# The last 64 rows of three weight matrices: sixteen long reads in place of 128 short ones

## The chip, the cores and the metric

The kernel runs on one core of a Trainium2 chip. The core has a matmul engine (PE, with PEld for its weight loads), a vector engine (DVE), an activation engine (ACT), a general engine (POOL) and a sequencer for transfers (SP), and sixteen DMA engines that move data between the chip's memory (HBM) and the on-chip memory (SBUF, 128 rows called partitions). The metric is the time of one launch in device microseconds, here as the median of three runs: lower is better.

## The reference

One decoding step for a batch of four: layer norm, attention of 32 query heads over a window of the last 4096 cached positions of 16 key/value heads, an output projection, a second norm and a gated feed-forward with ReLU as the gate. Cut to what is computed:

```python
B, Sq, D = 4, 1, 576;  Hq, Hkv, Sk, Dh = 32, 16, 16384, 128;  F = 4608;  W = 4096
xn = layernorm(x)
q = (xn @ wq)                                    # wq: 576 x 4096
k, v = k_cache[:, :, Sk - W:], v_cache[:, :, Sk - W:]    # each kv head serves two q heads
o = softmax(q k^T * Dh ** -0.5) v
h = x + o @ wo                                   # wo: 4096 x 576
hn = layernorm(h)
gate = hn @ W_gate;  gate = gate * (gate > 0)    # W_gate, W_up: 576 x 4608
h2 = h + (gate * (hn @ W_up)) @ W_down           # W_down: 4608 x 576
```

All tensors are bf16. Nearly all of the work is reading: the windows of K and V are 2 x 67 MB, the weights together some 25 MB. Every byte is read once.

## The kernel before

**Order by hand.** A small scheduler (class `Prog`) keeps one list of instructions for each engine and puts in semaphore waits from named dependencies. Nothing reorders the lists. All loads but that of x stand in SP's list; x's load and one of the two stores of the output are on ACT's.

**Memory.** One SBUF tensor `arena` (128 x 81,920 bf16) holds everything large. Its first 16,384 columns take q in a spread-out form, the rest are four slots of 16,384 columns (4 MB each). A load into a slot is issued by SP as soon as the last reader of what was there is done (`place`, L242, keeps an owner for every 64 columns). The loads in SP's order are: the last 64 rows of wq into `pp` (L251), its first 512 rows into a slot (L255), then K and V blocks of four heads each: K0 to K3, then K4, V0, K5, V1 and so on to K15, V11, then V12 to V15. After these come wo (L266), W_gate and W_up (L276), and W_down in five pieces (L282), laid over the arena as it falls free.

**Rows of the weights.** A weight of 576 rows is contracted in five chunks of 128 partitions. `main_rows` gives the first 512 rows to 128 partitions, four consecutive rows each, so a partition reads one contiguous run. `last_rows` gives the remaining 64 rows to 128 partitions by cutting each row in halves: partition 2r + a holds half a of row 512 + r. For wq that is a run of 2048 values (4,096 B) for each partition, for W_gate and W_up 2304 values (4,608 B). The matmuls use this layout through `xnT[:, 4:6]` and `hnT[:, 4:6]`, chunk 4 of the contraction, whose two columns are masked by `par` for even and odd partitions.

**Work.** PE projects q (L379 and L34, the helper `mm_same`). For each K block DVE transposes it in place (L422, 32 x 32 blocks), PE multiplies it with q (L446, L34); four blocks make a batch element, followed by a softmax (ACT and DVE). For each V block PE multiplies the weights with it (L507, L34) and DVE and ACT pick and add the heads' parts (L517 to L524). At the end come the output projection (L615), the second norm, the gate and up projections (L664, in the order W_gate, then W_up, chunk 4 first), the ReLU product and the down projection (L685), and two stores.

**What waits for the three loads.** wq's last rows (`("L", "wq", 1)`) are awaited by chunk 4 of the q projection, after the four main chunks. Those of W_gate (`("gu", 0, 4)`) and of W_up (`("gu", 1, 4)`) are issued ahead of the main part of the same matrix and are awaited by the first matmul of chunk 4 of that matrix.

Of the kernel before, what the change touches and what calls it, by code (L numbers as in the profile page):

```python
# [18 lines left out]
F = 4608  # L19
# [13 lines left out]
def mm_same(e, out, lhsT, rhs, start, stop, tile, pos):  # L33
    return e.add_instruction(mybir.InstMatmult(  # L34
        name=e.bass.get_next_instruction_name(), engine=mybir.EngineType.PE, ins=[e.lower_ap(rhs), e.lower_ap(lhsT)],
        outs=[e.lower_ap(out)], start_tensor_calc=start, stop_tensor_calc=stop, tile_size=tile, tile_position=pos,
        ldweights=False, bass_skip_group_check=True))


class Op:  # L40
# [80 lines left out]
def bass_sequential_preLN__sliding_block_cached__glu_gated_reglu__decode_kernel(  # L121
# [12 lines left out]
    with ExitStack() as es:  # L134
        cnt = [0]

        def sb(name, shape, dt):
            return es.enter_context(nc.sbuf_tensor("sb_" + name, shape, dt))

        P = Prog()  # L140
# [8 lines left out]
        arena = sb("arena", [128, AW], BF16)  # L149
# [44 lines left out]
        pT = pp[:, 0:4096]  # L194
# [21 lines left out]
        def place(name, off, size, reader, make, key=None):  # L216
            deps = []
            for blk in range(off // 64, (off + size) // 64):
                r = owner.get(blk)
                if r is not None and r not in deps:  # L220
                    deps.append(r)
                owner[blk] = reader
            semk = key or "d_" + "_".join(str(v) for v in name)
            P.dma("sync", ("L",) + name, make, semk, deps)
            land[name] = off
# [3 lines left out]
        def ring_slot():  # L229
            s = ring[0] % NSLOT  # L230
            ring[0] += 1
            return s
# [12 lines left out]
        def main_rows(W):  # L245
            return W[0:512, :].rearrange("(p r) n -> p (r n)", r=4)

        def last_rows(W):
            return W[512:576, :].rearrange("r (a n) -> (r a) n", a=2)

        P.dma("sync", ("L", "wq", 1), lambda e: e.dma_start(out=pT[:, 0:2048], in_=last_rows(A_wq)), "d_wq1")  # L251
        s = ring_slot()
        wq_off = slot0 + s * TILE
        place(("wq", 0), wq_off, TILE, "QMM",
# [12 lines left out]
        gu_off = {}  # L267
        off = WO_OFF + H * D
        for g, W in ((0, B_W_gate), (1, B_W_up)):
            for m, n, src in ((4, F // 2, last_rows(W)), (0, 3 * F, main_rows(W)[:, 0:3 * F]), (3, F, main_rows(W)[:, 3 * F:4 * F])):  # L270
                if g == 0 and m == 0:
                    n, src = 4 * F, main_rows(W)
                elif g == 0 and m == 3:
                    continue
                gu_off[(g, m)] = off
                place(("gu", g, m), off, n, ("GU", g, m), lambda e, off=off, n=n, src=src: e.dma_start(out=arena[:, off:off + n], in_=src))  # L276
                off += n
        WD_ROWS = (0, 15, 25, 32, 35, 36)
        wd_off = off
        for r0, r1 in zip(WD_ROWS, WD_ROWS[1:]):  # L280
            place(("wd", r0), wd_off + r0 * D, (r1 - r0) * D, ("DOWN", 1),
                  lambda e, r0=r0, r1=r1: e.dma_start(  # L282
                      out=arena[:, wd_off + r0 * D:wd_off + r1 * D],
                      in_=B_W_down.rearrange("(p r) n -> p (r n)", p=128)[:, r0 * D:r1 * D]))
# [18 lines left out]
                                                in_=c_qm[:, :, :].rearrange("p q (h j) -> p q h j", j=4),  # L303
# [4 lines left out]
                                                in_=to_v[:, :, :].rearrange("p n (k a) -> p n k a", a=4),  # L308
# [14 lines left out]
        for sg in range(2):  # L323
            pool(f"c_toq{sg + 1}", lambda e, sg=sg: e.affine_select(
                out=toq[:, :, :, :], in_=toq[:, :, :, :],
# [40 lines left out]
        def pe_q():  # L366
            for c in range(DC):
                for bk in range(2):
                    for g in range(4):
                        n = 4 * bk + g  # L370
                        w = arena[:, wq_off + c * H * DH + n * 512:][:, 0:512] if c < 4 else pT[:, g * 512:g * 512 + 512]
                        deps = []
                        if bk == g == 0:
                            deps = {0: [("L", "wq", 0), "xnT", "c_xnT"], 4: [("L", "wq", 1)]}.get(c, [])
                        if c < 4 and bk:
                            fn = lambda e, c=c, w=w, g=g, bk=bk: mm_same(e, bank[4 + bk][32 * g:32 * g + 32, :], xnT[:, c, :], w,
                                                                         c == 0, False, (128, 32), (0, 32 * g))
                        else:
                            fn = lambda e, c=c, w=w, g=g, bk=bk: e.matmul(  # L379
                                bank[4 + bk][32 * g:32 * g + 32, :], lhsT=xnT[:, c + bk if c == 4 else c, :], rhs=w,  # L380
                                start=(c == 0), stop=(c == 4), skip_group_check=True)
                        pe("QMM" if bk else "QMM0", fn, deps)
            for blk in range(8):
                pe("QT", lambda e, blk=blk: e.matmul(
                    bass.AP(tensor=psb, offset=7 * 512 + blk // 4 * 16 + blk % 4, ap=[[4096, 128], [4, 4], [32, 4]]),
                    lhsT=bass.AP(tensor=pp, offset=4096 + blk * 128, ap=[[PPW, 128], [1, 128]]),
                    rhs=bass.AP(tensor=ident_b, offset=0, ap=[[128, 128], [32, 4], [1, 4]]),
                    start=True, stop=True, skip_group_check=True), [f"qev{blk // 4}"] if blk % 4 == 0 else [])
# [36 lines left out]
        def pe_qk(g):  # L425
            b, qd = divmod(g, 4)
            for cb in range(4):
                for w in range(2):
                    for a in range(4):
                        deps = []  # L430
                        if cb == w == a == 0:
                            deps = [("TRA", g)]
                            if g == 0:
                                deps.append("QW")
                            if qd == 0 and b:
                                deps += [("EXP", b - 1), ("MAX", b - 1), ("EV", b - 1, 1)]
                        off = land[("K", g)] + w * QWW + cb // 2 * 64 + cb % 2 + a // 2 * 8 + a % 2 * 2
                        lhsT = arena[:, b * 2048 + cb * 512 + g % 4 * 128 + a * 32:][:, 0:32]
                        rhs = bass.AP(tensor=arena, offset=off, ap=[[AW, 128], [128, 64], [16, 4], [4, 2]])
                        out_ = bank[w][32 * a:32 * a + 32, :]  # L440
                        start, stop = g % 4 == cb == 0, g % 4 == cb == 3
                        if w:
                            fn = lambda e, a=a, out_=out_, lhsT=lhsT, rhs=rhs, start=start, stop=stop: mm_same(
                                e, out_, lhsT, rhs, start, stop, (128, 32), (0, 32 * a))
                        else:
                            fn = lambda e, out_=out_, lhsT=lhsT, rhs=rhs, start=start, stop=stop: e.matmul(  # L446
                                out_, lhsT=lhsT, rhs=rhs, start=start, stop=stop, skip_group_check=True)
                        pe(("QK", g), fn, deps)
# [90 lines left out]
        def finish_o():  # L539
            for q in range(4):  # L540
                for qd in range(4):
# [17 lines left out]
                                              in_=bass.AP(tensor=e8, offset=0, ap=[[8, 128], [0, 4], [1, 8]])), ["c_e8", "c_selc0"])  # L559
# [47 lines left out]
        for a in range(8):  # L607
            for n in range(2):
                for j in range(4):
# [4 lines left out]
                    else:  # L614
# [6 lines left out]
                                             in_=bass.AP(tensor=psb, offset=512 + 224, ap=[[4096, 128], [1, 64], [0, 2]])), ["part1"])  # L621
# [54 lines left out]
        for i in range(2):  # L676
            dve(("HHT", i), lambda e, i=i: e.transpose(
                out=hhT[:, 576 * i:576 * i + 576].rearrange("p (r q) -> p r q", q=32),
                in_=bass.AP(tensor=pp, offset=3712 + 18 * i, ap=[[PPW, 128], [1, 18], [36, 32]])), [("HH", m) for m in range(3)])
# [24 lines left out]
        for n in range(2):  # L704
            lo, hi = ncol[n]
            P.dma(("sync", "scalar")[n], ("O", n), lambda e, n=n, lo=lo, hi=hi: e.dma_start(
                out=orow[:, lo:hi], in_=out_sb[32 * n:32 * n + 4, 0:hi - lo]),
# [31 lines left out]
```

## Time and profile before

| what | value |
|---|---|
| median of 3 runs | 378.25 us (377.94 to 378.27) |
| span of the profiled execution | 376.5 us |
| DVE busy | 227.6 us (60%) |
| PE busy | 209.2 us (56%) |
| ACT busy | 53.8 us (14%) |
| mean DMA rate over the span | 424 GB/s |
| K loads, 16 of 4096 KB, issue to landing | 26.2 us (median) |
| V loads, 16 of 4096 KB, issue to landing | 28.5 us (median) |
| wq, first 512 rows, issued at 1.3 us | lands 12.9 us later |
| W_gate, first 512 rows, issued at 320.1 us | lands 29.3 us later |
| x, 4.5 KB, on ACT's queue, issued at 0.93 us | lands at 3.66 us |
| first matmul of the q projection (L379) | 14.21 us |
| first matmul of the gate projection (L664) | 353.56 us |

How to read the profile: one execution is recorded, and times are microseconds from the start of its span. The runs' times are taken without the profiler and by another clock, which takes in what lies around the span; they are close to it but not the same. "Landing" is the time when the last of the sixteen DMA engines has marked its share of a load as done. A DMA engine takes the shares of one queue in the order of their issue, each as a number of packets; the trace has start and duration of every packet, without the engine's number. "Busy" of an engine says nothing by itself: what counts is which wait ends last.

### The profile page before, as it was taken

The page shows a single profiled execution, that of the slowest core. Times are in us where ns is not written, and L with a number is a line of the kernel's source. Part 1 is how long each engine was busy: PE and PEld are TensorE (multiplying, and loading weights), DVE is VectorE, ACT ScalarE, POOL GpSimd, SP SyncE. Part 2 cuts the span into 40 slices and gives each one's busy share as a digit, 9 for nine tenths or more (in the row PEclk, how much of TensorE's full clock was granted, in tenths as well). Part 3 has the DMA queues.
Part 4 walks back from the last instruction along what each step waited for, and adds up shares of the span by engine and source line. Part 5 has one row for each costly group of instructions (what it writes and reads, how often), then busy time and mean ns, then how long its engine had stood idle before and what let it go on. Part 6 is the DMA issues. An engine that isn't in the chain of part 4 may idle for free.

```text
span 376.5 us, 2541 instructions
## 1 busy us (share of the span) xinstructions
PE 209.2 (56%) x1447; PEld 39.2 (10%) x694; DVE 227.6 (60%) x164; ACT 53.8 (14%) x84; POOL 10.7 (3%) x29
## 2 busy tenths in 40 slices
PE   0404443249919091749282844664555687776748
PEld 0000000001101010101010100110000101003305
DVE  3088878779292959584847778665659423342140
ACT  3093000211000114010101140101010401121010
POOL 8300000000000000000000000000000000000000
PEclk9975666659979687788778885968596989996688
DMA  8999999999999999999999999999999999999996
GB/s 335 446 435 432 413 446 446 425 411 446 444 421 414 443 444 421 414 446 446 421 413 446 446 418 421 438 446 418 425 439 446 413 432 435 430 423 426 437 414 263
DMA packets 6514, 159.74 MB, mean 424 GB/s; under 512 B 736, under 2 KB 872, under 8 KB 1512
## 3 DMA queue, kind: packets, MB, share of 16 engines
q1 hardware_dynamic: 6488, 159.58, 98.8%
q8 instruction: 8, 0.13, 0.1%
q10 hardware_dynamic: 16, 0.01, 0.0%
q14 instruction: 2, 0.02, 0.0%
HBM read 159.58 MB, written 0.00 MB: 424 GB/s over the span
## 4 chain that ended last, share of the span: by engine, by line
DMA 62%; DVE 18%; PE 18%; SPq 1%; issue 1%; ACT 0%
DMA sb_arena<-in_A_k_cache_dram 53%; DVE sb_arena L422 16%; PE psb L34 11%; DMA sb_arena<-in_B_W_down_dram 9%; PE psb L446 4%; PE psb L507 2%; DVE sb_o_tmp L520 1%; DVE sb_pp L485 1%; PE psb L685 0%; SPq L242 0%; PE psb L473 0%; SPq L282 0%; ACT sb_out_sb L702 0%; SPq L255 0%; SPq L251 0%
## 5 line engine op out<-in xcount | busy, mean ns | idle before, releaser
L422 DVE STREAM_TRANSPOSE sb_arena<-sb_arena 128x8192 f32<-128x8192 f32 (+1 forms) x19 | 139.9, 7365 | 66.5 <-DMA sb_arena<-in_A_k_cache_dram 66.5
L446 PE MATMUL psb<-sb_arena 128*32 128x512 bf16 x256 | 42.5, 629 | 119.1 <-DVE sb_arena L422 119.0
L34 PE MATMUL psb<-sb_arena,sb_pp 128*128 128x512 bf16 x382 | 105.2, 383 | 2.7 <-issue 2.6
L507 PE MATMUL psb<-sb_arena,sb_pp 128*128 128x512 bf16 x115 | 44.1, 383 | 8.9 <-DVE sb_o_tmp L520 8.9
L34 PE MATMUL psb<-sb_arena 128*32 128x512 bf16 x256 | 44.2, 649 | 0.0
L517 ACT COPY sb_o_tmp<-psb 32x512 f32<-32x512 f32 x32 | 18.5, 577 | 179.3 <-PE psb L34 179.1
L520 DVE TENSOR_TENSOR sb_o_tmp<-psb,sb_fm 32x512 f32<-32x512 f32 x32 | 21.7, 678 | 16.9 <-PE psb L34 16.4
L446 PEld LDWEIGHTS psb<-sb_arena 128*32 128x32 bf16 x256 | 9.6, 119 | 161.4 <-DVE sb_arena L422 132.2
L507 PEld LDWEIGHTS psb<-sb_arena,sb_pp 128*128 128x128 bf16 x128 | 12.6, 99 | 113.4 <-issue 113.4
L524 DVE TENSOR_REDUCE sb_o_sel<-sb_o_tmp 128x128 f32<-128x512 f32 x16 | 17.7, 1106 | 0.5
L465 ACT ACTIVATE sb_pp<-psb,sb_hx 128x1024 bf16<-128x1024 f32 x4 | 4.5, 1113 | 78.4 <-DVE sb_hx L462 78.4
L485 DVE TENSOR_TENSOR sb_pp<-psb,sb_m 128x1024 bf16<-128x1024 f32 x8 | 9.4, 1209 | 4.5 <-PE psb L473 4.5
L480 ACT ACTIVATE sb_pp<-psb,sb_m 128x512 bf16<-128x512 f32 x16 | 9.7, 692 | 14.8 <-PE psb L473 14.8
L523 DVE TENSOR_TENSOR sb_o_tmp<-sb_o_tmp,sb_fm 64x512 f32<-64x512 f32 x16 | 11.0, 690 | 0.5
L413 ACT COPY sb_arena<-sb_q_keep 32x256 bf16<-32x256 bf16 x8 | 9.7, 1452 | 0.1
L685 PE MATMUL psb<-sb_arena,sb_pp 128*32 128x352 bf16 (+1 forms) x72 | 7.6, 349 | 3.7 <-DMA sb_arena<-in_B_W_down_dram 3.6
L399 DVE CAST sb_pp<-psb 128x512 bf16<-128x512 f32 x1 | 2.4, 2426 | 11.3 <-PE psb L379 11.3
L468 DVE STREAM_TRANSPOSE sb_pp<-sb_pp 128x1024 bf16<-128x1024 bf16 x4 | 5.0, 1246 | 5.1 <-ACT sb_pp L465 5.1
L473 PE MATMUL psb<-sb_pp,sb_to_v 128*32 128x256 bf16 x64 | 4.3, 401 | 6.2 <-DVE sb_pp L468 6.2
L673 DVE TENSOR_TENSOR sb_pp<-psb,sb_pp 128x384 bf16<-128x384 f32 x3 | 1.5, 551 | 9.0 <-PE psb L664 9.0
L379 PE MATMUL psb<-sb_arena,sb_xnT 128*32 128x512 bf16 x16 | 2.6, 628 | 7.2 <-DMA sb_arena<-in_A_wq_dram 7.2
L664 PE MATMUL psb<-sb_arena,sb_hnT 128*32 128x384 bf16 x40 | 4.2, 405 | 3.9 <-DVE sb_hnT L645 2.0
(119 smaller groups left out, 88.1 us busy)
## 6 DMA issues: line engine op xcount, KB each, us to landing
sb_arena<-in_A_k_cache_dram SPq DMA_DIRECT2D x16, 4096.0 KB, 26.2
sb_arena<-in_A_v_cache_dram SPq DMA_DIRECT2D x16, 4096.0 KB, 28.5
sb_arena<-in_A_wo_dram SPq DMA_DIRECT2D x1, 4608.0 KB, 26.2
sb_arena<-in_B_W_gate_dram SPq DMA_DIRECT2D x1, 4608.0 KB, 29.3
sb_arena<-in_A_wq_dram SPq DMA_DIRECT2D x1, 4096.0 KB, 12.9
sb_arena<-in_B_W_up_dram SPq DMA_DIRECT2D x1, 3456.0 KB, 30.3
sb_arena<-in_B_W_down_dram SPq DMA_DIRECT2D x1, 2160.0 KB, 29.6
sb_arena<-in_B_W_down_dram SPq DMA_DIRECT2D x1, 1440.0 KB, 32.6
```

Source lines behind the costliest of these rows:

```text
L34: return e.add_instruction(mybir.InstMatmult(name=e.bass.get_next_instruction_name(), engine=mybir.EngineType.PE, ins=[e.lower_ap(rhs), e. ...
L413: act("QW", lambda e, i=i, q=q: e.copy(out=bass.AP(tensor=arena, offset=32 * i * AW + 2 * i + q, ap=[[AW, 32], [512, 16], [136, 4], [32, 4]]),
L422: dve(("TRA", g), lambda e: e.transpose(out=dst, in_=src), [("L", "K", g)] if lo == 0 else [])
L446: fn = lambda e, out_=out_, lhsT=lhsT, rhs=rhs, start=start, stop=stop: e.matmul(out_, lhsT=lhsT, rhs=rhs, start=start, stop=stop, skip_gr ...
L480: act(("EV", b, 0), lambda e, a=a: e.activation(out=bass.AP(tensor=pp, offset=2 * a, ap=[[PPW, 128], [8, 2], [32, 128], [1, 2]]), in_=bank ...
L485: dve(("EV", b, 1), lambda e, n=n: e.tensor_tensor(out=bass.AP(tensor=pp, offset=16 + 8 * n, ap=[[PPW, 128], [32, 128], [2, 4], [1, 2]]), ...
L507: fn = lambda e, lhsT=lhsT, rhs=rhs, k=k, j=j: e.matmul(bank[2 + j], lhsT=lhsT, rhs=rhs, start=(k == 0), stop=(k == 7), skip_group_check=True)
L517: act(("OSC", g), lambda e, j=j: e.copy(out=o_tmp[32 * j:32 * j + 32, 0:512], in_=bank[2 + j][32 * j:32 * j + 32, :]), [("PV", g), ("OSEL" ...
L520: dve(("OSD", g), lambda e, j=j: e.tensor_tensor(out=ot(32 * j, 32), in0=bank[2 + j][32 * j:32 * j + 32, :].rearrange("p (t d) -> p t d", ...
L523: dve(("OS", g), lambda e: e.tensor_tensor(out=ot(64, 64), in0=ot(64, 64), in1=fmb(64, 64), op=ALU.mult), [("OSC", g)])
L524: dve(("OSEL", g), lambda e: e.tensor_reduce(out=o_sel[:, qd, b, :], in_=o_tmp[:, 0:512].rearrange("p (t d) -> p d t", d=DH), axis=AX.X, o ...
L685: return lambda e: e.matmul(bank[n][32 * n:32 * n + 32, 0:hi - lo], lhsT=lhsT, rhs=w[:, lo:hi], start=start, stop=stop, skip_group_check=True)
```

## The change

Three loads are written differently: the last 64 rows of wq (L251), of W_gate and of W_up (L276, those with m = 4). The 64 rows lie in HBM as one contiguous stretch. Before, both sides of the transfer are 128 runs of half a row. After, the source is sixteen runs of four whole rows (32,768 B for wq, 36,864 B for W_gate and W_up), while the destination is still 128 partitions of a half row each, so one source run fills eight neighbouring partitions. Since partition 2r + a holds half a of row r, the bytes lie in SBUF exactly where they lay. The two sides now differ in shape, and a new helper `load_wide` adds the copy instruction directly, on SP's queue. Semaphores, waits, the order of issue and all other loads are as they were.

```diff
+def load_wide(e, out, in_):
+    return e.add_instruction(mybir.InstDMACopy(
+        name=e.bass.get_next_instruction_name(), engine=mybir.EngineType.SP, mode="Copy", queue="qSPDynamicHW",
+        ins=e.lower_ap_dma(in_), outs=e.lower_ap_dma(out)))
...
-        def last_rows(W):
-            return W[512:576, :].rearrange("r (a n) -> (r a) n", a=2)
-
-        P.dma("sync", ("L", "wq", 1), lambda e: e.dma_start(out=pT[:, 0:2048], in_=last_rows(A_wq)), "d_wq1")
+        def last_wide(W):
+            n = W.shape[1]
+            return bass.AP(tensor=W.tensor, offset=512 * n, ap=[[4 * n, 16], [1, 4 * n]])
+
+        P.dma("sync", ("L", "wq", 1), lambda e: load_wide(e, pT[:, 0:2048], last_wide(A_wq)), "d_wq1")
...
-            for m, n, src in ((4, F // 2, last_rows(W)), (0, 3 * F, main_rows(W)[:, 0:3 * F]), (3, F, main_rows(W)[:, 3 * F:4 * F])):
+            for m, n, src in ((4, F // 2, last_wide(W)), (0, 3 * F, main_rows(W)[:, 0:3 * F]), (3, F, main_rows(W)[:, 3 * F:4 * F])):
...
-                place(("gu", g, m), off, n, ("GU", g, m), lambda e, off=off, n=n, src=src: e.dma_start(out=arena[:, off:off + n], in_=src))
+                place(("gu", g, m), off, n, ("GU", g, m), lambda e, off=off, n=n, src=src, m=m: (
+                    load_wide(e, arena[:, off:off + n], src) if m == 4 else e.dma_start(out=arena[:, off:off + n], in_=src)))
```

## The prediction

> **What bounds the kernel now.** I read the page first: its slices, its DMA queues and its chain of waits.
>
> ```profile
> span 376.5 us, 2541 instructions
> ...
> DMA  8999999999999999999999999999999999999996
> GB/s 335 446 435 432 413 446 446 425 411 446 444 421 414 443 444 421 414 446 446 421 413 446 446 418 421 438 446 418 425 439 446 413 432 435 430 423 426 437 414 263
> ...
> q1 hardware_dynamic: 6488, 159.58, 98.8%
> q8 instruction: 8, 0.13, 0.1%
> ...
> DMA 62%; DVE 18%; PE 18%; SPq 1%; issue 1%; ACT 0%
> ```
>
> The reader should see that the 16 DMA engines are busy at 90% or more in 38 of 40 slices, and that the one queue SP fills (q1) accounts for 98.8% of their time. 159.58 MB at the rate of the long middle stage (below: 431 GB/s) is 370 us of 376.5. The chain names DVE and PE too, but they stand there because a slot is refilled only when its reader is done; loads wait about 26 us in the queue after issue (next views), so the DMA engines never run dry over it. A microsecond lost in the DMA stream anywhere is a microsecond at the end.
>
> Second, the stretch from the last weights to the end, in the chain in order of time, and what PE waited for there:
>
> ```profile
> 338.23 34.60 DMA sb_arena<-in_B_W_down_dram
> 372.83 0.04 issue
> 372.88 1.86 PE psb L685 x19
> 374.74 0.02 issue
> 374.76 0.44 ACT sb_out_sb L702
> ```
>
> ```profile
> PE psb L685 <- DMA sb_arena<-in_B_W_down_dram: 3.6, 1, 3.6
> ...
> PE psb L664 <- DMA sb_arena<-in_B_W_up_dram: 1.9, 2, 1.1
> ```
>
> PE stands waiting for W_up and W_down as they land. The last piece lands at 374.26; what comes after it is 2.2 us, which the change does not touch.
>
> Third, the three loads in question and their neighbours (size in KB, us from issue to landing), and the rate by stage (PE, PEld, DVE, ACT, POOL busy, clock, DMA share, GB/s).
>
> ```profile
> sb_arena<-in_A_wo_dram SPq DMA_DIRECT2D x1, 4608.0 KB, 26.2
> ...
> sb_arena<-in_B_W_gate_dram SPq DMA_DIRECT2D x1, 576.0 KB, 27.2
> sb_arena<-in_B_W_up_dram SPq DMA_DIRECT2D x1, 576.0 KB, 30.4
> sb_pp<-in_A_wq_dram SPq DMA_DIRECT2D x1, 512.0 KB, 3.6
> ```
>
> ```profile
> 1.80:2.30 0.50, 0.00 (x0) 0.00 (x0) 0.00 (x0) 0.48 (x2) 0.35 (x2) 1.00 1.00 164
> 2.30:2.60 0.30, 0.00 (x0) 0.00 (x0) 0.19 (x1) 0.00 (x0) 0.30 (x2) 1.00 0.60 232
> ...
> 90.00:310.00 220.00, 131.19 (x784) 18.32 (x327) 144.79 (x91) 25.65 (x45) 0.00 (x0) 0.80 1.00 431
> ```
>
> wo is issued at 310.96 and lands at 337.12; W_gate's last rows, right behind it in the queue, land at 338.54: 1.42 us for 589,824 B. W_up's land 1.41 us after the load ahead of them (350.87 against 349.46). wq's last rows start the stream: first packet at 1.85, last engine done at about 4.1, while the queue ran at 164 to 232 GB/s.
>
> **The change, part by part.** Bytes, semaphores, waits, order of issue and place of every byte in SBUF are unchanged. Three loads change form: sixteen reads of 32,768 B (wq) or 36,864 B (gate, up) in place of 128 of 4,096 B or 4,608 B, and an engine then writes eight neighbouring rows.
>
> (1) *Fewer reads.* By the packet records one 4,096 B packet takes 159 ns, a 32,768 B one 1,216, a 36,864 B one 1,368: about 37 ns per KB plus 8 ns a packet, 27 GB/s an engine at either size. Inside wq's load packets follow each other every 155 ns, so eight are 1.24 us against 1.21: −0.03. At 431 GB/s 589,824 B are 1.37 us against the 1.42 and 1.41 seen: −0.05 and −0.04. In all −0.12 us. That is the whole gain the rows can show; read length hardly matters here.
>
> (2) *Writes by other engines.* What the trace of before does not show is a load in which an engine writes eight neighbouring rows. All big loads use one assignment of rows to engines and run at 27 GB/s an engine whatever the packet size, so the limit lies in the engine or where it writes. If nothing on the writing side is shared, the cost is nothing: the lower bound is part (1), −0.12. If two engines at a time go to one place that takes 27 GB/s, the load takes twice its time: 524,288 B and twice 589,824 B at 431 GB/s are 1.22 + 1.37 + 1.37 = 3.96 us more. The nearest rows where streams disturb each other: wq's cold load, 2.25 us for 1.22 us of bytes (1.8 times), and an instruction packet (16 KB, q8) on one engine, which took 1.08 us with 1.68 us for the 32 KB packet behind it: 2.76 us for 0.61 + 1.22 = 1.83 (1.5 times). These rows lie nearer to two than to one, so I take two: +3.96 − 0.12 = **+3.8 us**, and keep both ends. A worse end is possible: at the end of the stream the 16 engines are 1.74 us apart (first and last completion mark of the last load, 372.52 and 374.26). An engine early in gate's or up's load may then write where a late engine still writes the previous one, and that late engine is the one that sets the end. Charging once more the 1.37 us of each of these two gives +2.7, so +6.5 as the outer bound.
>
> [...]
>
> (3) *Issue on SP.* The old issues took 0.41 us (L251) and 0.33 to 0.43 (L276). The new form isn't in the trace; between the 0.33 of wo and the 0.69 of the longest K issue it adds −0.1 to +0.3 us on SP. Behind the first one stands wq's main load, whose issue ends at 1.67 and whose first packet starts at 3.47: 1.8 us of cover. Behind the other two stand loads that wait for PE until 320.1 and 328.8. Cost nothing; if the first cover were gone, 0.3.
>
> (4) *The x load*, on ACT's queue, has its four packets between wq's at 2.85 to 3.07, and four engines stand about 0.5 us over it. With one packet per engine it may wait for the packet's end, about 3.5 in place of 2.85, and x lands about 0.6 later than 3.66. DVE's bn_stats (L337) waits for it, behind it the norm and PE's transposes, ready at 7.4; PE then waits till 14.2 for wq: 6.8 us of cover, so nothing.
>
> (5) *Where a stall goes.* wq's loss delays the K loads behind it; W_gate's and W_up's are covered for their own readers (W_gate's last rows land at 338.54, first read at 353.56) but not for what stands behind them: W_up's main part and W_down land later by the sum, PE waits on just these, and the 2.2 us after the last landing follow.
>
> **Sum.** 376.5 + 3.8 = 380.3 for the profiled span. The page gives no time outside the span; the runs' median, 378.25, is 1.75 above it and I carry that over: 380.3 + 1.75 = **382.1 us**. With the doubling only partly in force (half of it, +1.9) it is 380.1; the forecast's own range is 379.5 to 383.
>
> **Rivals.**
> A, *no sharing on the write side*: part (1) alone, 378.25 − 0.12 = 378.1, no measurable change. For it: engines run independently, each at its own 27 GB/s, with no packet of a steady load stretched by another engine's. Against it: these loads all have one assignment, so they can't show it. A load that is split back into rows of 4 KB when issued, the change not doing what it says, gives the same: 378.25.
> B, *the start gets shorter*, the case on the other side: place, the first 2.3 us, where the queue runs at 164 to 232 GB/s because each engine pays the first latency (packets of 0.56 to 0.66 us in place of 0.16), and four stand 0.5 us over x. If one read per engine pays that once, an engine needs 0.5 + 1.22 = 1.7 us from its start, 1.85 to 2.1, and the last is done at about 3.6 to 3.8 in place of 4.1: −0.3 to −0.5, −0.8 if x's stall goes as well; with gate and up −0.4 to −0.9: 377.6. It decides if writes meet no obstacle and the four late engines are those that end last. For it: starts 0.6 us apart survive to the first K landing (23.34 to 23.88). Against it: the ends differ more by which engine got an instruction packet.
> C, *engines out of step obstruct neighbours*: the outer bound, +5 to +6.5, about 384. For it the 1.74 us; against, only part of these engines can meet.
>
> **How the numbers follow.** Forecast 0.42, A 0.20, B 0.20, C 0.18. About 0.2% (0.76 us) is what can be told from no change. Faster by over that takes the better half of B's cases and cases in which the last engines gain most, 0.18; within it, A and the rest of B with a little of the partial doubling, 0.22; slower, C and nearly all of the forecast, 0.60. The time is the forecast's, 382.1. The range takes in A, the forecast, most of B and about half of C: 377.4 to 384.2; the forecast alone is 379.5 to 383.
>
> **What would show it.** Right: W_gate's last rows land about 2.7 us after wo rather than 1.42, W_up's likewise after W_gate's, the first load's last mark near 5.5 rather than 4.44, the first K landing late by over a microsecond; the middle stage stays at 431 GB/s and the tail at 2.2 us. Wrong: these gaps stay at 1.37 to 1.42 (A), or the first landing comes before 4.1 with the gaps unchanged (B). A change of rate in the K and V loads, or a tail longer than 2.2 us, would break the premise that only these three loads count.

## The result, and the profile after

The changed kernel takes 384.12 us (median of 5 runs, 383.85 to 385.52) against 378.27 us (377.94 to 378.50) for the kernel before on the same chip: ratio 1.016, 95% interval 1.0146 to 1.0173. It is 5.85 us slower. The forecast was 382.1 us and its range ended at 384.2, so the result lies at its very edge: the direction was right, the loss was put a third too low.

The page of the changed kernel, the lines that answer to those of before:

```profile
span 382.8 us, 2541 instructions
...
DMA  8999999999999999999999999999999999999996
GB/s 329 404 435 435 423 438 438 435 438 431 406 438 431 432 433 438 431 435 411 435 437 428 438 435 432 426 431 418 438 431 437 435 438 425 445 312 360 359 418 249
...
q1 hardware_dynamic: 6152, 159.58, 98.6%
...
DMA 57%; PE 21%; DVE 20%; issue 1%; SPq 1%; ACT 0%
```

The reader should look at the two rows together. The busy digits are 9 in 38 of 40 slices, as before, and the bytes are the same, but three slices near the end carry 312, 360 and 359 GB/s where the kernel before had 423, 426 and 437. The DMA engines are as busy as ever and move less. A busy share alone would have hidden the loss. Packets fell by 336, which is 3 x 112: 16 reads for 128 in each of the three loads.

By stage (PE, PEld, DVE, ACT, POOL busy, clock, DMA share, GB/s), first the kernel before, then the changed one:

```profile
20.00:300.00 280.00, 149.73 (x962) 22.02 (x430) 199.58 (x109) 38.59 (x60) 0.00 (x0) 0.76 1.00 431
...
334.00:345.00 11.00, 7.34 (x84) 2.45 (x55) 3.36 (x5) 2.64 (x4) 0.00 (x0) 0.77 1.00 429
...
350.00:358.00 8.00, 5.52 (x73) 1.88 (x28) 1.72 (x11) 0.26 (x2) 0.00 (x0) 0.57 0.99 425
```

```profile
20.00:300.00 280.00, 149.56 (x962) 22.23 (x430) 198.84 (x108) 38.00 (x58) 0.00 (x0) 0.80 1.00 432
...
334.00:345.00 11.00, 7.71 (x63) 1.50 (x39) 4.45 (x6) 2.64 (x4) 0.00 (x0) 1.00 0.98 325
...
350.00:358.00 8.00, 5.32 (x42) 3.59 (x26) 1.87 (x12) 0.20 (x1) 0.00 (x0) 0.67 0.98 273
```

The long middle stage is untouched (431 and 432). The two stretches around the new loads fall from 429 to 325 and from 425 to 273 GB/s at a DMA share of 0.98.

Where the time went is read from the landings, one load after the other in the order of the queue:

| last landing of | before | after | step before | step after | more |
|---|---|---|---|---|---|
| V15 | 326.19 | 327.18 | | | 0.99 (from the start) |
| wo (form unchanged) | 337.12 | 339.64 | 10.93 | 12.46 | 1.53 |
| W_gate, last rows | 338.54 | 342.11 | 1.42 | 2.47 | 1.05 |
| W_gate, main (unchanged) | 349.46 | 354.48 | 10.92 | 12.37 | 1.45 |
| W_up, last rows | 350.87 | 357.48 | 1.41 | 3.00 | 1.59 |
| W_up, 3 of 4 main rows (unchanged) | 359.08 | 365.44 | 8.21 | 7.96 | −0.25 |
| W_down, last piece | 374.26 | 380.62 | 15.18 | 15.18 | 0.00 |

The column adds up to 6.36 us, 380.62 less 374.26. That is 0.5 more than the 5.85 between the medians. A run's time was 1.2 to 1.3 us above its profiled span in every later kernel; by that the profiled execution of the kernel before (span 376.5) stands for some 377.7 to 377.8 us, below the fastest of its runs here. Nearly half of the column, 2.98 us, is in wo and W_gate's main part, the loads that stand just ahead of the changed ones and have not been changed. By the packet records, packets of 36,864 B all took near 1,370 ns before, but for one behind an instruction packet (1,861 ns). Now those of the changed loads take 2,024 to 3,004 ns, and the last ones of the late engines in the loads just ahead take up to some 2,450. The load behind a changed one, W_up's main rows, loses nothing in its step (7.96 us, where it was 8.21).

After the last landing nothing changed, as the end of the chain in order of time shows (start us, us, what):

```profile
341.71 37.48 DMA sb_arena<-in_B_W_down_dram
379.19 0.04 issue
379.23 1.85 PE psb L693 x19
381.09 0.02 issue
381.11 0.44 ACT sb_out_sb L710
```

### The profile page after: what moved, and what is told of

Its sections match the earlier page's. It is cut to its first block, busy times and chain, and to the rows that moved or that the text cites. A ratio compares the mean times of both kernels' runs of the same rounds, so it can differ in the third digit from the quotient of the medians.

```text
span 382.8 us, 2541 instructions
## 1 busy us (share of the span) xinstructions
PE 211.5 (55%) x1447; PEld 39.0 (10%) x694; DVE 228.8 (60%) x164; ACT 53.7 (14%) x84; POOL 10.5 (3%) x29
## 4 chain that ended last, share of the span: by engine, by line
DMA 57%; PE 21%; DVE 20%; issue 1%; SPq 1%; ACT 0%
DMA sb_arena<-in_A_k_cache_dram 47%; DVE sb_arena L430 16%; PE psb L34 13%; DMA sb_arena<-in_B_W_down_dram 10%; PE psb L454 4%; PE psb L515 3%; DVE sb_o_tmp L528 1%; DVE sb_pp L493 1%; PE psb L481 1%; PE psb L693 0%; DVE sb_pp L476 0%; DVE sb_hx L459 0%; ACT sb_pp L473 0%; SPq L290 0%; SPq L41 0%
## 5 line engine op out<-in xcount | busy, mean ns | idle before, releaser
L34 PE MATMUL psb<-sb_arena,sb_pp 128*128 128x512 bf16 x382 | 107.3, 389 | 2.9 <-issue 2.8
L515 PE MATMUL psb<-sb_arena,sb_pp 128*128 128x512 bf16 x115 | 44.8, 390 | 9.0 <-DVE sb_o_tmp L528 9.0
L672 PE MATMUL psb<-sb_arena,sb_hnT 128*32 128x384 bf16 x40 | 5.0, 481 | 6.7 <-DMA sb_arena<-in_B_W_up_dram 4.7
L34 PE MATMUL psb<-sb_arena,sb_hnT 128*32 128x384 bf16 x80 | 7.7, 476 | 0.0
```

The source lines that it names most:

```text
L34: return e.add_instruction(mybir.InstMatmult(name=e.bass.get_next_instruction_name(), engine=mybir.EngineType.PE, ins=[e.lower_ap(rhs), e. ...
L515: fn = lambda e, lhsT=lhsT, rhs=rhs, k=k, j=j: e.matmul(bank[2 + j], lhsT=lhsT, rhs=rhs, start=(k == 0), stop=(k == 7), skip_group_check=True)
```

## The experiments

In the code shown here, "..." stands for lines left out, such as those that put wq back to its old form. Two theories were set against each other. *Shared write place*, the author's assumption: sixteen source runs against 128 rows give each DMA engine eight neighbouring rows, two engines at a time then write to one place that takes no more than one engine moved before, 27 GB/s (36,864 B in 1,368 ns), and the load runs at half rate. Which rows an engine gets is inferred from the grouping; the trace does not number the engines, and no run shows such a place. *Long read*: one read that feeds eight writes holds its engine up. A third question was why the loss is more than a doubling of three short loads.

**One part alone: wq.** W_gate and W_up go back to the old form.

```diff
-            for m, n, src in ((4, F // 2, last_wide(W)), ...
+            for m, n, src in ((4, F // 2, last_rows(W)), ...
...
```

> Only wq's last rows in the new form, W_gate's and W_up's as before. The changed kernel's first K landing came 0.69 us later (24.57 against 23.88) and V15's 0.99 us later. If the three loads' costs simply add, this kernel is 0.7 to 1.0 us slower than before: about 379.1 us. If wq's load only shifts the engines against each other and its cost vanishes behind the later loads, it is within 0.3 us of 378.3.

Measured: 378.95 us against 377.90, ratio 1.0027 (1.0018 to 1.0036), 1.05 us more. The cost of wq's load is not hidden by what follows.

**The other part alone: W_gate and W_up.**

```diff
-        P.dma("sync", ("L", "wq", 1), lambda e: load_wide(e, pT[:, 0:2048], last_wide(A_wq)), "d_wq1")
+        P.dma("sync", ("L", "wq", 1), lambda e: e.dma_start(out=pT[:, 0:2048], in_=last_rows(A_wq)), "d_wq1")
```

> Only W_gate's and W_up's last rows in the new form, wq's as before. If the costs add: 5.0 to 5.4 us slower than before, about 383.5 us, which is 2.5 to 2.7 us for a load of 1.37 us. If each load merely takes its own time twice, as the forecast had it, and the rest came from engines that wq had put out of step: 2.7 us slower, about 381.0 us.

Measured: 382.56 us, ratio 1.0124 (1.011 to 1.0138), 4.66 us more. With wq's 1.05 that is 5.71, close to the 5.85 of the whole change: the parts add. Engines put out of step by wq explain little. 4.66 us for two loads is far above the 2.7 of a plain doubling.

**Short reads, eight rows an engine.** The source is cut into 4,608 B again, but grouped 16 x 8; wq as before.

```diff
-            return bass.AP(tensor=W.tensor, offset=512 * n, ap=[[4 * n, 16], [1, 4 * n]])
+            return bass.AP(tensor=W.tensor, offset=512 * n, ap=[[4 * n, 16], [n // 2, 8], [1, n // 2]])
...
```

> As the run with W_gate and W_up alone, but the source is read in 128 runs of 4,608 B, grouped 16 x 8, so that each engine still writes eight neighbouring rows. Theory 'shared write place': the reads' length is no matter, the same loss as with long reads, 5 us, about 383.5 us, with the packets of these loads at 4,608 B and longer than 179 ns. Theory 'long read': one read that feeds eight writes holds the engine up, so short reads lose nothing: 378.3 us.

Measured: 382.36 us, ratio 1.0115 (1.0102 to 1.0129), 4.46 us more. The packets of 4,608 B took 303 ns on average, where those of the kernel before took 180. The same two stretches in this kernel:

```profile
334.00:345.00 11.00, 7.35 (x69) 1.53 (x46) 4.03 (x6) 2.64 (x4) 0.00 (x0) 1.00 0.98 328
...
350.00:358.00 8.00, 5.53 (x49) 3.23 (x28) 1.72 (x11) 0.21 (x1) 0.00 (x0) 0.62 0.95 305
```

328 and 305 GB/s with reads as short as before. The long read is not the cause; that theory falls.

**32 runs in place of 16.** By the grouping an engine now has two runs of 18,432 B, each for four neighbouring rows; wq as before.

```diff
-            return bass.AP(tensor=W.tensor, offset=512 * n, ap=[[4 * n, 16], [1, 4 * n]])
+            return bass.AP(tensor=W.tensor, offset=512 * n, ap=[[2 * n, 32], [1, 2 * n]])
...
```

> W_gate's and W_up's last rows read in 32 runs of 18,432 B, two runs an engine, each feeding four neighbouring rows; wq as before. The K loads, whose source is grouped 32 x 4, run at full rate. Theory 'shared write place': if the two runs of an engine are apart as they must be in the K loads, no two engines meet and the time is 378.2 us, up to 0.1 below before; if they are neighbours, 5 us slower as with 16. Theory 'long read' (one read feeding several writes): a loss of 2 to 4 us, since a read still feeds four writes.

Measured: 378.10 us against 377.90, ratio 1.0007 (0.9998 to 1.0016): no loss or gain that can be told. The same stretches:

```profile
334.00:345.00 11.00, 7.35 (x84) 1.85 (x53) 3.36 (x5) 2.64 (x4) 0.00 (x0) 0.96 1.00 429
...
350.00:358.00 8.00, 5.53 (x60) 2.33 (x28) 1.71 (x11) 0.20 (x1) 0.00 (x0) 0.57 0.99 423
```

429 and 423, as before the change. The reads are four times as long as the writes, the instruction is added by the same helper and the two sides differ in shape; none of this costs anything. What costs is the grouping into sixteen. On the first theory the two runs of an engine must then lie apart in SBUF, which the trace can't show.

**The suspected cost, eight times as large.** wo keeps its reads of 36,864 B, grouped 16 x 8; all else as before.

```diff
-              lambda e: e.dma_start(out=arena[:, WO_OFF:WO_OFF + H * D], in_=A_wo.rearrange("(p r) n -> p (r n)", p=128)))
+              lambda e: load_wide(e, bass.AP(tensor=arena, offset=WO_OFF, ap=[[AW, 128], [1, 1], [1, H * D]]),
+                                  bass.AP(tensor=A_wo.tensor, offset=0, ap=[[8 * H * D, 16], [H * D, 8], [1, H * D]])))
```

> Only the load of wo changes, 4,718,592 B: read in 128 runs of 36,864 B as before, grouped 16 x 8, so that an engine writes eight neighbouring rows; W_gate, W_up and wq as before. Theory 'two engines share one place of 27 GB/s all through': the load takes 10.9 us more, and with 1 to 2 us for engines that stand in their neighbours' way, 12 us: about 390 us. Theory 'a loss at the change-over alone, whatever the size': 2 to 2.5 us, about 380.5 us, since engines drift apart until pairs take turns.

Measured: 390.62 us against 378.07, ratio 1.0342 (1.0314 to 1.0369), 12.55 us more. Four stretches inside this load, in a profile of the slowest of the four runs (392.63 us):

```profile
326.00:332.00 6.00, 4.39 (x21) 0.46 (x5) 3.03 (x4) 1.15 (x2) 0.00 (x0) 1.00 0.99 203
332.00:338.00 6.00, 5.48 (x26) 0.51 (x6) 0.54 (x2) 0.48 (x1) 0.00 (x0) 1.00 1.09 233
338.00:344.00 6.00, 1.93 (x32) 1.38 (x32) 2.88 (x5) 2.16 (x4) 0.00 (x0) 0.70 1.04 215
344.00:350.00 6.00, 0.00 (x0) 0.00 (x0) 0.00 (x0) 0.00 (x0) 0.00 (x0) 0.50 0.82 178
```

203 to 233 GB/s at full DMA share: half of 431. A row counts a packet by its start, so rows as short as these are rough, and the last one, in which the first engines finish, shows 178 at a share of 0.82. The packets say it best: all 106 of this load that start between 326 and 344 us took 2.68 to 3.57 us, median 2.84, where such a packet took 1.37 before. The loss does not fade as the load goes on, as it would have if engines had drifted into taking turns.

**Cut by rows, in the old form.** W_gate's and W_up's last rows as two ordinary loads each, one for partitions 0 to 63 and one for 64 to 127.

```diff
...
+                    place(("gu", g, "lo"), off, n, ("GU", g, m), lambda e, off=off, n=n, src=src: e.dma_start(out=arena[0:64, off:off + n], in_=src[0:64]))
+                    P.dma("sync", ("L", "gu", g, m), lambda e, off=off, n=n, src=src: e.dma_start(out=arena[64:128, off:off + n], in_=src[64:128]), f"d_gu_{g}_{m}")
...
```

> W_gate's and W_up's last rows in the old form and with reads of 4,608 B, but each as two loads, one to partitions 0 to 63 and one to 64 to 127. If what counts is how many places the 16 engines write at a time (64 partitions are half of the places), each load runs at half rate: 2.7 us slower at least, with obstructed neighbours about 5: 381 to 383 us. If only the new form of the instruction, with its two sides of unequal shape, costs time: 378.0 to 378.2 us.

**Cut by columns.** The control: two loads each, all 128 partitions with half of the columns.

```diff
...
+                    place(("gu", g, "lo"), off, n, ("GU", g, m), lambda e, off=off, n=n, src=src: e.dma_start(out=arena[:, off:off + n // 2], in_=src[:, 0:n // 2]))
+                    P.dma("sync", ("L", "gu", g, m), lambda e, off=off, n=n, src=src: e.dma_start(out=arena[:, off + n // 2:off + n], in_=src[:, n // 2:n]), f"d_gu_{g}_{m}")
...
```

> The control to the row halves: the same two loads each, but cut by columns, 128 partitions with 2,304 B each. All places are in use at any time, so there is no loss but that of packets: 16 in place of 8 an engine at 8 ns, twice, plus completion marks, 0.1 to 0.2 us: 378.1 us on either theory. A loss of some us would mean that the number of loads matters by itself.

Measured: cut by rows 383.81 us, ratio 1.0156 (1.0136 to 1.0176), 5.74 us more and so above the expected 381 to 383; cut by columns 378.00 us, ratio 1.0001 (0.9992 to 1.0011). The stretch with the first of these loads, by rows and then by columns:

```profile
332.00:338.00 6.00, 5.83 (x27) 0.74 (x8) 1.72 (x2) 0.00 (x0) 0.00 (x0) 1.00 1.04 331
```

```profile
332.00:338.00 6.00, 5.87 (x27) 0.78 (x8) 1.69 (x2) 0.00 (x0) 0.00 (x0) 1.00 1.06 441
```

331 against 441 GB/s with the same number of loads and the same instruction. By rows, the packets of 4,608 B took 308 ns on average, where those of the kernel before took 180. Loads to 64 partitions lose as those with sixteen groups do (308 and 303 ns for a packet of 4,608 B), and the new instruction is not needed for it. The number of loads is no matter. Nor do fewer engines do the work: each half load leaves sixteen completion marks. A cause on the reading side was not tried by itself. Against it speaks that the row halves read the same runs of HBM, of the same 4,608 B, as the kernel before.

**W_gate alone.** Of the change, only W_gate's load.

```diff
...
+                place(("gu", g, m), off, n, ("GU", g, m), lambda e, off=off, n=n, src=src, m=m, g=g: (
+                    load_wide(e, arena[:, off:off + n], src) if m == 4 and g == 0 else e.dma_start(out=arena[:, off:off + n], in_=src)))
```

> Of the changed kernel only W_gate's load in the new form. Both together cost 4.67 us on their own. If each costs the same: 2.3 us, about 380.2 us. If the second one costs more since it meets engines that the first has put out of step: 1.4 to 1.9 us, 379.3 to 379.8 us.

Measured: 381.06 us (380.05 to 381.83), ratio 1.0077 (1.0054 to 1.0099): 2.0 to 3.7 us. This holds the equal share of 2.3 and leaves out the 1.4 to 1.9 of the other theory, but its runs lie too far apart to say more. In its profile, of the fastest run, wo ahead of the changed load takes 12.42 us in place of 10.93, and W_gate's main part behind it 10.69, no more than the 10.92 of before.

**Two change-overs fewer.** W_gate and W_up in the new form, W_up's last rows issued directly behind W_gate's. A change-over is a place in the queue where a load of one grouping follows a load of the other.

```diff
...
+        for g, m, o, n, src in (gu[0], gu[2], gu[1], gu[3], gu[4]):
+            place(("gu", g, m), o, n, ("GU", g, m), ...
```

> As the run with W_gate and W_up alone in the new form (4.67 us slower), but W_up's last rows issued directly behind W_gate's, ahead of W_gate's main part. Theory 'half of the loss is neighbours obstructed at each change of assignment': two changes in place of four, so about 1.0 to 1.5 us less loss: 3.0 to 3.7 us, 381.0 to 381.7. Theory 'each such load costs 2.3 us wherever it stands': 382.6 again.

Measured: 381.49 us against 378.22, ratio 1.0087 (1.0074 to 1.01), 3.27 us more in place of 4.66. The same two loads of the same form, with two changes of assignment in the queue in place of four, lose 1.4 us less. So part of the loss sits at the change-overs. In its profile wo, ahead of both, takes 12.30 us, and W_gate's main part, now behind both, 10.66: by these steps it is the load ahead of a change that loses here (10.93 before), not the one behind (10.92 before).

**All three in 32 runs**, the candidate for a version that beats both, with the edit shown for 32 runs applied to wq too.

> All three loads in 32 runs of two rows (16,384 B for wq, 18,432 B for W_gate and W_up). With W_gate and W_up so the time was that of before (ratio 1.0007, 0.9998 to 1.0016). If the shared places were the whole loss, wq's load costs nothing either: 378.0 us, 0.2 either way. If part of the changed kernel's 0.9 us at the start comes from the instruction's longer issue (0.60 in place of 0.41 us, first packet 0.3 later): 378.3 to 378.5.

Measured: 378.42 us against 378.22, ratio 1.0007 (0.9999 to 1.0016). wq's load in this form lands at 4.49, as before (4.44). It is no better than the kernel before. Between the two expectations, 378.0 give or take 0.2 and 378.3 to 378.5, the interval can't decide: it runs from 0 to 0.6 us longer than before.

**x behind wq.** The kernel before, with x loaded through SP's queue.

```diff
-        P.dma("scalar", ("L", "x"), lambda e: e.dma_start(out=x_bf[:, :], in_=A_x.rearrange("b s d -> (b s) d")), "d_x")
+        P.dma("sync", ("L", "x"), lambda e: e.dma_start(out=x_bf[:, :], in_=A_x.rearrange("b s d -> (b s) d")), "d_x")
```

> The kernel before with one edit: x is loaded through SP's queue, behind wq's last rows, in place of ACT's. The rival on the start said that the 0.5 us that four engines lose over x could be had back. If these are the engines that end last: 0.3 to 0.5 us faster, 377.6. If others end last: the same time, 378.0. If x's later landing (4.5 in place of 3.66) mattered, slower; PE has 6.8 us of cover, so not expected.

Measured: 379.06 us, ratio 1.0032 (1.0017 to 1.0047), slower. The 12 runs lie between 377.80 and 380.56; the profiled one is the fastest of them, and its last weights land at 374.27, as before. It shows no gain at the start. Why the other runs are 0.3 to 2.8 us longer this profile can't show, and it stays open.

## Why the prediction was right or wrong

**What bounds the kernel: right.** The DMA stream sets the end. 6.36 us lost between the first load and the last piece of W_down are 6.3 us of span (382.8 against 376.5), and 2.2 us follow the last landing in both. One reading was loose: the 26 us that loads were said to wait in the queue run from issue to landing, and nearly 10 of them are the load's own transfer (4096 KB at 431 GB/s).

**(1) Fewer reads: right, as far as it can be told.** 0.12 us at most was expected. 32 runs have a quarter of the reads and show 1.0007 (0.9998 to 1.0016), and the two loads land 1.43 and 1.40 us behind the one ahead, where it was 1.42 and 1.41: nothing.

**(2) Writes by other engines: the doubling right, the size wrong.** This is the step that failed. The prediction took "two" from a choice between no cost and a doubling, and the wo run shows the two: 2.84 us for a packet that took 1.37. The rows it leaned on for that, a cold load and an instruction packet, show no engines that write to one place; that they pointed to two was luck. But the prediction charged the doubling to the three loads' own bytes alone, +3.96, and put the engines that get in their neighbours' way at nothing in the forecast: they stood only in the outer bound (+6.5 in all) and in a rival of chance 0.18. The runs show that this loss belongs in the forecast. For W_gate and W_up together the doubling is 2.74 us and the runs give 4.66, so by this estimate some 1.9 us are neighbours' loss, about 1 us for each of the two changes into the new form; with the two loads side by side and one such change, 3.27 − 2.74 leaves 0.5. In the landings it shows as 1.53 us in wo and 1.45 in W_gate's main part, each just ahead of a changed load. The two splits differ, since part of the changed load already moves while the load ahead still has to land: W_gate's first packet of 36,864 B in the new form starts at 335.67, wo's last mark is at 339.64.

Why the load ahead loses is argued, not shown: its engines finish up to 1.8 us apart (wo's first and last mark, 335.36 and 337.12), longer than the 1.4 us of a changed load, so an early engine in the new assignment can write where a late one still writes the load ahead. The stretched last packets of the late engines fit this, but the trace does not say which engine met which.

For wq, 1.22 us was expected and 1.05 measured, but the number agrees better than its parts: its sixteen packets took 1.37 to 2.11 us, not the 2.43 of a doubling, and its first one came 0.32 us later. Rival C, +5 to +6.5, was the right size.

No run shows the place that two engines share, which the +3.96 was worked out from, nor that all big loads of before give the same rows to the same engines; both were the author's assumptions. What the runs show in its place is the rate. wo grouped 16 x 8 ran at 203 to 233 GB/s in the three full stretches, where the long middle stage of before ran at 431. Packets of 4,608 B took 303 ns grouped 16 x 8 and 308 ns in halves of 64 partitions, in place of 180. Groupings by four lose nothing: the K loads are grouped so in the 431 GB/s of the middle stage, and the stretches with the 32 runs show 429 and 423 where it was 429 and 425. Which rows lie in one place, if any do, was not tried row by row.

**(3) Issue on SP: nearly right.** wq's new issue took 0.60 us in place of 0.41 and its first packet came at 2.17 in place of 1.85. The prediction looked only at the cover behind that issue; the first load of all has none ahead of it. The 0.3 us it named for that case was there at the first packet. Whether it costs time stays open: in the 32 runs for all three loads the first packet also came late (2.23), yet wq's load landed as before.

**(4) The x load: right that it costs nothing, wrong on the way.** x was expected 0.6 us later and came 1.26 earlier (2.40 in place of 3.66), since wq's first packets started after it (2.17, where x's four start at 1.88 to 1.94). The four engines no longer stood over x, and the kernel was slower all the same.

**(5) Where the stall goes: right.** PE now stands 4.7 us for W_up at once, as what it waited for in the last stretch shows (us in total, times, longest):

```profile
PE psb L672 <- DMA sb_arena<-in_B_W_up_dram: 4.7, 1, 4.7
PE psb L693 <- DMA sb_arena<-in_B_W_down_dram: 3.3, 2, 2.9
```

Before it was 1.9 and 3.6 us. W_gate's last rows, landing 3.6 us later, were still 11 us ahead of their reader at the old time of 353.56.

**The rivals.** A (no sharing) fell with the wo run. B (a shorter start) fell with wq alone, 1.05 us slower. Of the signs named, W_gate's last rows 2.7 us behind wo came as 2.47, W_up's behind W_gate's main part as 3.00, the first load's last mark near 5.5 as 5.33; the first K landing was 0.69 us late, not over a microsecond.

**The sum.** To reach the time of a run, the prediction added 1.75 us to the span, the median less the one profiled span it had. In every later kernel a run's time is 1.2 to 1.3 us above its own span (384.12 against 382.8 here). So some 0.5 us of the 382.1 came from comparing a median with a fast execution, and in the span itself the forecast fell 2.5 us short (380.3 against 382.8), not 2.0.

## What to carry to other kernels

The grouping of a load mattered more here than the length of its reads: with its source in sixteen groups against 128 partitions wo ran at 203 to 233 GB/s in place of 431, at a DMA share of 0.99 to 1.09, and with 64 partitions only, a packet took 308 ns in place of 180; in 32 groups the two stretches kept 429 and 423 GB/s. That the grouping sets which engine writes which rows is the author's reading; the runs do not show the engines one by one. Read the rate beside the busy share. In this queue, busy at 90% or more in 38 of 40 slices, a load in another grouping also slowed the load ahead of it (wo 12.46 us in place of 10.93, W_gate's main part 12.37 in place of 10.92), so price that as well as its own bytes.

## What was not expected of the hardware

Loads in the same queue that were not changed at all lost time to a neighbour: wo took 12.46 us in place of 10.93. The forecast had left this out. And the half rate lasted: with wo grouped 16 x 8, every one of its packets that start between 326 and 344 us took 2.68 us or more in place of 1.37. Which engines held each other up, if any did, the trace does not show.
